# Attention, then a leaky-ReLU MLP, on one core: rebuilding how the attention stage gets its transposed state, its column sums and its evacuations

## Chip, cores, metric

One core of one Trainium2 chip. The metric is the device time of one execution in microseconds (us), median over executions of the same kernel. The engines are named as in the profile: PE (TensorE, the matmuls), ACT (ScalarE), DVE (VectorE), GpSimd, and SyncE, which here only issues transfers. PSUM is where this kernel's matmuls put their results (`ps` in the profile's lines). Before the change: 412.0 us (16 runs, 410.8 to 413.2).

## The reference, cut to what matters

```python
B, H, S, Ns, D = 8, 8, 512, 32, 64           # 64 heads in all
scores  = x @ state.T / 8;  a  = softmax(scores);   xread = a @ state      # (512 x 32) per head
scores2 = state @ x.T / 8;  a2 = softmax(scores2);  sread = a2 @ x         # (32 x 512) per head
tok = concat([xread, sread], axis=2)         # -> 4352 tokens x 512
h = tok @ w_in;  g = max(0.01 * h, h);  out = g @ w_out                    # d_ff = 2048
```

Both softmaxes use the same exponentials, so the kernel computes exp(scores) once per head, in four tiles of 128 tokens.

## The kernel before

Five engine programs with semaphores; the listing is shortened and mostly in comments. Heads run through a software pipeline: step `w` works on head `w` in A, `w-1` in E, and so on.

```python
def dma_hbm_batch(b):      # on GpSimd: x -> xs, state -> ss (both bf16 in HBM), x -> Xbf in SBUF
def dma_sbuf_batch(b):     # on SyncE, nine transfers on one semaphore, sem_in[b]
    # waits for xs[b] and ss[b], then
    #   XTp[c] <- xs, c = 0..3   DMA transpose, 128 x 512
    #   STp[c] <- ss, c = 0..3   DMA transpose, 128 x 32
    #   Sall   <- ss             plain load
# PE, per head:
# A  4 matmuls  scores           (waits sem_in[b] >= 9*16, sem_xbf[b])
# B  4 matmuls  sread numerator  (weights Xbf, 64 columns)
#    4 matmuls  its denominator  (weights ones64, 64 columns)
# C  4 transposes of normalised E2n;  D 1 matmul  xread, 512 columns
# ACT: E 4 exps with accumulator output (the row sums);  G copy ET <- PSUM (32x512 bf16)
# DVE: F reciprocal, product E2n;  H reciprocal and product for sread;  I cast X2T <- PSUM (64x512 fp32)
...
dma_hbm_batch(0); dma_hbm_batch(1); dma_hbm_batch(2)
dma_sbuf_batch(0); dma_sbuf_batch(1)
dma_weights()              # W1 (4 loads) and W2 (4 loads), all at the start
dma_sbuf_batch(2)
for w in range(NH_ALL + 7): # A(w) B(w-2) C(w-3) D(w-5) | E(w-1) G(w-4) | F(w-2) H(w-3) I(w-6)
    ...                    # batch b >= 3 is loaded after D of the last head of batch b-3 (three buffers)
# second stage: per group of 512 tokens 64 matmuls (mm1, L387), leaky ReLU on ACT + DVE, 64 matmuls (mm2, L426)
```

The softmax here doesn't subtract the row's maximum and nothing guards it: scores larger than these inputs give would overflow.

## Time and profile before

| | before |
|---|---|
| time, median | 412.0 us |
| first A (scores matmul of head 0) | 26.0 us |
| last A (head 63) | 160.1 us |
| first matmul of the second stage | 169.2 us |
| second stage | 242.1 us |
| a head, A to A, inside a batch | 1.853 us |

The span is read in two pieces: the attention up to the first mm1 matmul, and the second stage, which the change leaves alone. Inside the attention the starts of A tell everything: the distance from one to the next is the period, and a longer one in front of a batch is a hole. The lines are in the prediction. "x4" after a line of the timeline means that four instructions of a kind are merged into it.

### The profile page before, as it was taken

What the parts mean: (1) busy time and instruction counts of PE and PEld (TensorE: products, weight loads), DVE (VectorE), ACT (ScalarE), POOL (GpSimd) and SP (SyncE); (2) the same over time, 40 slices, a digit from 0 to 9 for tenths busy, and PEclk for the clock granted to TensorE, in tenths of its full rate; (3) what the DMA queues carried; (4) which work ended last, traced back from release to release, by engine and by line L of the source; (5) the groups of instructions that cost most, each with busy time, mean ns of one, the idle gap of its engine ahead of it and who ended that gap; (6) DMA issues with size and microseconds to landing.
All of it is one profiled execution on the core that took longest, in us unless ns stands there. A gap on an engine that the chain in (4) does not pass through costs nothing.

```text
span 411.4 us, 6534 instructions
## 1 busy us (share of the span) xinstructions
PE 356.5 (87%) x2186; PEld 174.4 (42%) x2208; DVE 194.6 (47%) x464; ACT 190.9 (46%) x755; POOL 40.2 (10%) x39
## 2 busy tenths in 40 slices
PE   0046939599689979899999999999999999999996
PEld 0034625365455646233443444434434434344542
DVE  0025838488658868478408137064082270550600
ACT  1045727377557756266326245164262461542511
POOL 7550211221404000000000000000000000000000
DMA  9999999929999900000020110200201101102022
GB/s 67 157 156 198 185 169 128 123 48 141 81 102 83 84 6 2 2 2 0 25 78 0 53 51 1 78 25 24 75 5 41 63 1 60 44 1 77 26 78 76
DMA packets 95425, 26.91 MB, mean 65 GB/s; under 512 B 88224, under 2 KB 90528, under 8 KB 95392
## 3 DMA queue, kind: packets, MB, share of 16 engines
q0 software_dynamic: 70656, 12.85, 38.8%
q1 hardware_dynamic: 24736, 13.64, 14.8%
q8 instruction: 18, 0.29, 0.3%
q14 instruction: 15, 0.12, 0.1%
HBM read 25.95 MB, written 13.37 MB: 96 GB/s over the span
## 4 chain that ended last, share of the span: by engine, by line
PE 73%; SPq 17%; DMA 7%; issue 1%; POOL 1%; DVE 0%; ACT 0%; POOLq 0%; ACTq 0%
PE ps L387 29%; PE ps L426 28%; SPq L166 9%; SPq L172 7%; DMA Sall<-ss 5%; PE ps L297 5%; PE ps L277 4%; PE ps L257 3%; PE ps L215 2%; DMA ss<-in_state_dram 2%; PE ps L264 2%; POOL xs L141 0%; DVE X2T L317 0%; SPq L177 0%; ACT OB L441 0%
## 5 line engine op out<-in xcount | busy, mean ns | idle before, releaser
L408 DVE SCALAR_TENSOR_TENSOR G<-Hs 128x512 bf16<-128x512 bf16 (+1 forms) x144 | 95.4, 663 | 124.4 <-ACT Hs L401 122.8
L387 PE MATMUL ps<-X2T,W 128*128 128x512 bf16 (+1 forms) x565 | 121.9, 373 | 2.1 <-DVE X2T L317 1.4
L426 PE MATMUL ps<-W,G 128*128 128x512 bf16 x533 | 118.0, 379 | 0.6
L401 ACT CAST Hs<-ps 128x512 bf16<-128x512 f32 (+1 forms) x144 | 80.9, 562 | 43.3 <-PE ps L387 42.9
L426 PEld LDWEIGHTS ps<-W,G 128*128 128x128 bf16 x544 | 53.1, 98 | 64.1
L387 PEld LDWEIGHTS ps<-X2T,W 128*128 128x128 bf16 x576 | 48.0, 99 | 75.1 <-ACT Hs L401 36.2
L441 ACT COPY OB<-ps 128x512 f32<-128x512 f32 x34 | 19.9, 585 | 97.7 <-PE ps L426 97.7
L230 ACT ACTIVATE E2s<-ps 128x32 bf16<-128x32 f32 x192 | 35.4, 194 | 58.5 <-PE ps L264 34.1
L215 PE MATMUL ps<-STp,XTp 64*128 64x32 bf16 x256 | 17.9, 189 | 48.0 <-DMA Sall<-ss 48.0
L317 DVE CAST X2T<-ps 64x512 bf16<-64x512 f32 x64 | 43.7, 683 | 2.5 <-PE ps L297 0.4
L290 ACT COPY ET<-ps 32x512 bf16<-32x512 bf16 x64 | 36.7, 573 | 17.5 <-PE ps L297 16.8
L215 PEld LDWEIGHTS ps<-STp,XTp 64*128 64x128 bf16 x256 | 11.5, 104 | 74.1 <-issue 49.6
L297 PE MATMUL ps<-ET,Sall 32*64 32x512 bf16 x64 | 40.1, 630 | 0.4 <-DVE X2T L317 0.4
L277 PE MATMUL ps<-ident,E2n 128*32 128x128 bf16 x256 | 39.0, 308 | 0.0
L247 DVE TENSOR_TENSOR E2n<-E2s,RD 128x128 bf16<-128x128 bf16 x64 | 18.7, 292 | 36.2 <-PE ps L277 35.8
L230 ACT ACTIVATION_READ_ACCUMULATOR E2s<-ps 128x1 f32 x192 | 35.3, 203 | 0.0
L257 PE MATMUL ps<-E2s,Xbf 128*64 128x32 bf16 x256 | 25.2, 219 | 0.6 <-ACT E2s L233 0.6
L141 POOL DMA_DIRECT2D xs<-in_x_dram x8 | 16.6, 2078 | 83.7 <-PE ps L215 81.6
L242 DVE RECIPROCAL RD<-DEN 128x4 bf16<-128x4 f32 x64 | 10.8, 169 | 28.3 <-ACT E2s L233 27.4
L264 PE MATMUL ps<-E2s,ones 128*64 128x32 bf16 x256 | 23.9, 214 | 0.0
L277 PEld LDWEIGHTS ps<-ident,E2n 128*32 128x32 bf16 x256 | 21.9, 129 | 2.8 <-DVE RC L306 0.4
L306 DVE RECIPROCAL RC<-ps 64x32 f32<-64x32 f32 x64 | 21.9, 342 | 0.2 <-PE ps L297 0.2
(18 smaller groups left out, 118.0 us busy)
## 6 DMA issues: line engine op xcount, KB each, us to landing
out_dram<-OB SPq DMA_DIRECT2D x34, 256.0 KB, 2.0
xs<-in_x_dram POOLq DMA_DIRECT2D x8, 512.0 KB, 8.6
Xbf<-in_x_dram POOLq DMA_DIRECT2D x8, 512.0 KB, 10.2
W<-in_moe_w_in_dram POOLq DMA_DIRECT2D x4, 512.0 KB, 20.7
W<-in_moe_w_out_dram POOLq DMA_DIRECT2D x4, 512.0 KB, 31.1
XTp<-xs SPq DMA_TRANSPOSE x32, 4.4
STp<-ss SPq DMA_TRANSPOSE x32, 5.7
...
```

The source lines that it names most:

```text
L166: P_sp.emit(lambda b=b, c=c, bs=bs: sync.dma_start(out=XTp[bs][c].ap(), in_=xs[b][:, c * 128:(c + 1) * 128], transpose=True,).then_inc(sem ...
L215: return pe.matmul(reg_sc(q)[:, 32 * t:32 * t + 32], XTp[bs][ct].ap()[hd:hd + 64, 128 * t:128 * t + 128], STp[bs][ct].ap()[hd:hd + 64, 0:32],)
L230: P_act.emit(lambda t=t, p=p, q=q: act.activation(E2s[p].ap()[:, t, :], reg_sc(q)[:, 32 * t:32 * t + 32], AF.Exp, scale=SCALE, accum_out=D ...
L257: return pe.matmul(reg_srn(q), Xbf[bs].ap()[:, h, t, :], E2s[p].ap()[:, t, :], start=(t == 0), stop=(t == 3))
L277: return pe.transpose(out=reg_et(p)[:, 128 * t:128 * t + 128], in_=E2n[p].ap()[:, t, :], identity=ident.ap(),)
L290: T[i]["etec"] = P_act.mark(lambda p=p: act.copy(ET[p].ap(), reg_et(p)))
L297: T[i]["xrd"] = P_pe.mark(lambda bs=bs, h=h, p=p: pe.matmul(psX[p].ap()[0:64, 0:512], Sall[bs].ap()[:, h, :], ET[p].ap()))
L317: T[i]["xrec"] = P_dve.mark(lambda p=p, ct=ct, hd=hd, tokc=tokc: dve.tensor_copy(X2T[ct].ap()[hd:hd + 64, tokc:tokc + NS], psX[p].ap()[0:6 ...
L387: return pe.matmul(psM1[q].ap()[:, 0:ntok], W1[c].ap()[:, ft * 128:(ft + 1) * 128], X2T[c].ap()[:, tok0:tok0 + ntok], start=(c == 0), stop ...
L401: hc = P_act.mark(lambda q=q, ntok=ntok: act.copy(Hs[q].ap()[:, 0:ntok], psM1[q].ap()[:, 0:ntok]))
L408: e = P_dve.mark(lambda gi=gi, ft=ft, q=q, ntok=ntok: dve.scalar_tensor_tensor(G[gi % 2][ft].ap()[:, 0:ntok], Hs[q].ap()[:, 0:ntok], 0.01, ...
L426: return pe.matmul(psM2[m].ap()[:, 0:512], G[gi % 2][c].ap()[:, rc * 128:rc * 128 + 128], W2[c // 4].ap()[:, c % 4, :], start=(c == 0), st ...
```

## The change

The intent: take the state's transposes off the SyncE queue, let a head wait only for what it needs, and lighten all three compute engines in the attention. In words:

- Sall is loaded straight from HBM by GpSimd; STp is made by a PE transpose of Sall (Tst) and an ACT copy (Q), once per two heads. SyncE issues only the four XTp transposes, each with its own semaphore.
- Xbf gets 64 columns of ones beside its 64 columns of x (Xone), so four matmuls with 128-column weights give numerator and denominator at once.
- One exp of 128 columns per head in place of four with accumulator output; the row sums come from a DVE reduce, and reduce, reciprocal and product run once per two heads.
- The ET copy goes from ACT to DVE, the 64x512 cast from DVE to ACT.
- W2's four loads go from the start to behind batches 3 to 6.
- To make the pairs possible, C runs one step later (`w-4` in place of `w-3`), and H, G and F stand at the front of a step.

The diff is condensed: "..." marks what is cut, and loops are put on one line.

```diff
-        P_sp.wait(sem_ss[b], 16)
         for c in range(4):
-            ...XTp...  .then_inc(sem_in[b], 16))
-        for c in range(4):
-            ...STp[bs][c] <- ss, transpose=True...
-        ...Sall[bs] <- ss...
+            ...XTp...  .then_inc(sem_xt[b][c], 16))
...
+    def grp_Tst(i):                      # PE, even heads
+        T[i]["stt"] = P_pe.mark(... pe.transpose(out=reg_stt(q),
+            in_=Sall[bs].ap()[:, 2 * ct:2 * ct + 2, :], identity=ident.ap()[0:32, 0:32]))
+    def grp_Q(i):                        # ACT
+        T[i]["q"] = P_act.mark(... act.copy(STps[bs][ct].ap(), reg_stt(q)))
...
-        P_pe.wait(sem_in[b], IN_PER_BATCH)
-        P_pe.wait(sem_xbf[b], 16)
+        P_pe.wait(sem_xt[b][ct], 16)
+        P_pe.wait(P_act.sem, ev("q", i - (i % 2)))
...
-        for t in range(4): pe.matmul(reg_srn(q), Xbf[bs].ap()[:, h, t, :], E2s[p].ap()[:, t, :], ...)
-        for t in range(4): pe.matmul(reg_d2r(q), ones64.ap(), E2s[p].ap()[:, t, :], ...)
+        for t in range(4): pe.matmul(reg_sr2(q), Xone[bs].ap()[:, h, t, :], E2s[pp].ap()[:, tk + t, :], ...)
...
-        T[i]["etec"] = P_act.mark(... act.copy(ET[p].ap(), reg_et(p)))
+        T[i]["g"] = P_dve.mark(... dve.tensor_copy(ET[p].ap(), reg_et(p)))
...
-        T[i]["xrec"] = P_dve.mark(... dve.tensor_copy(X2T..., psX[p].ap()[0:64, 0:512]))
+        T[i]["xev"] = P_act.mark(... act.copy(X2T..., psX[p].ap()[0:64, 0:512]))
...
+                if bb < 7:
+                    dma_w2(bb - 3)       # one W2 load behind each of batches 3 to 6
```

More of the change, by code (lines that the diff above doesn't have):

```diff
@@ L8 @@
 ALU = mybir.AluOpType
+AX = mybir.AxisListType
 NB, NH, NS, NSS, ND = 8, 8, 512, 32, 64
@@ L19 @@
 NBANK_C = 4
+NH_ALL = NB * NH
 class _Prog:
@@ L27, in __init__ @@
         self.count = 0
-        self.emitted = 0
         self.ops = []
@@ L32, in emit, with mark @@
         self.ops.append(fn)
-    def ticket(self):
+    def mark(self, fn):
         self.count += 1
-        return self.count
-    def mark(self, fn, ticket=None):
-        if ticket is None:
-            ticket = self.ticket()
-        self.emitted += 1
-        assert ticket == self.emitted, (ticket, self.emitted)
         sem = self.sem
@@ L48, in mark @@
         self.ops.append(_go)
-        return ticket
+        return self.count
     def wait(self, sem, value):
@@ L73, in bass_block_recurrent_cross__then__act_leaky_relu_kernel @@
     ss = nc.dram_tensor("ss", [NB, NSS, D_MODEL], DT.bfloat16)
-    Xbf = [nc.alloc_sbuf_tensor(f"Xbf{i}", [128, NH, 4, ND], DT.bfloat16) for i in range(NBUF_B)]
+    Xone = [nc.alloc_sbuf_tensor(f"Xone{i}", [128, NH, 4, 128], DT.bfloat16) for i in range(NBUF_B)]
+    Sall = [nc.alloc_sbuf_tensor(f"Sall{i}", [NSS, NH, ND], DT.bfloat16) for i in range(NBUF_B)]
     XTp = [[nc.alloc_sbuf_tensor(f"XTp{i}_{c}", [128, NS], DT.bfloat16) for c in range(4)]
            for i in range(NBUF_B)]
-    STp = [[nc.alloc_sbuf_tensor(f"STp{i}_{c}", [128, NSS], DT.bfloat16) for c in range(4)]
-           for i in range(NBUF_B)]
-    Sall = [nc.alloc_sbuf_tensor(f"Sall{i}", [NSS, NH, ND], DT.bfloat16) for i in range(NBUF_B)]
-    E2s = [nc.alloc_sbuf_tensor(f"E2s{i}", [128, 4, 32], DT.bfloat16) for i in range(2)]
-    DEN1 = [nc.alloc_sbuf_tensor(f"DEN1_{i}", [128, 4], DT.float32) for i in range(2)]
-    RD1 = [nc.alloc_sbuf_tensor(f"RD1_{i}", [128, 4], DT.bfloat16) for i in range(2)]
-    E2n = [nc.alloc_sbuf_tensor(f"E2n{i}", [128, 4, 32], DT.bfloat16) for i in range(2)]
-    ET = [nc.alloc_sbuf_tensor(f"ET{i}", [32, 512], DT.bfloat16) for i in range(2)]
+    STps = [[nc.alloc_sbuf_tensor(f"STps{i}_{c}", [128, NSS], DT.bfloat16) for c in range(4)]
+            for i in range(NBUF_B)]
+    E2s = [nc.alloc_sbuf_tensor(f"E2s{i}", [128, 8, 32], DT.bfloat16) for i in range(2)]
+    DEN1 = [nc.alloc_sbuf_tensor(f"DEN1_{i}", [128, 8], DT.float32) for i in range(2)]
+    RD1 = [nc.alloc_sbuf_tensor(f"RD1_{i}", [128, 8], DT.bfloat16) for i in range(2)]
+    E2n = [nc.alloc_sbuf_tensor(f"E2n{i}", [128, 8, 32], DT.bfloat16) for i in range(2)]
+    ET = [nc.alloc_sbuf_tensor(f"ET{i}", [32, NS], DT.bfloat16) for i in range(2)]
     RC2 = [nc.alloc_sbuf_tensor(f"RC2_{i}", [64, 32], DT.float32) for i in range(2)]
-    ones64 = nc.alloc_sbuf_tensor("ones64", [128, 64], DT.bfloat16)
     X2T = [nc.alloc_sbuf_tensor(f"X2T{i}", [128, N_TOK], DT.bfloat16) for i in range(4)]
@@ L106, in reg_sc, with reg_sr2, reg_stt @@
         return psC[q].ap()[:, 0:128]
-    def reg_srn(q):
-        return psC[q].ap()[0:64, 128:160]
-    def reg_d2r(q):
-        return psC[q].ap()[0:64, 160:192]
+    def reg_sr2(q):
+        return psC[q].ap()[:, 128:160]
+    def reg_stt(q):
+        return psC[q].ap()[:, 224:240].bitcast(DT.bfloat16)
     def reg_et(p):
@@ L125, in bass_block_recurrent_cross__then__act_leaky_relu_kernel, with ev @@
     sem_ss = [nc.alloc_semaphore(f"sem_ss{b}") for b in range(NB)]
+    sem_sal = [nc.alloc_semaphore(f"sem_sal{b}") for b in range(NB)]
     sem_xbf = [nc.alloc_semaphore(f"sem_xbf{b}") for b in range(NB)]
-    sem_in = [nc.alloc_semaphore(f"sem_in{b}") for b in range(NB)]
+    sem_xt = [[nc.alloc_semaphore(f"sem_xt{b}_{c}") for c in range(4)] for b in range(NB)]
     sem_ob = [nc.alloc_semaphore(f"sem_ob{i}") for i in range(2)]
-    def ev_of(T, name, i):
+    T = [{} for _ in range(NH_ALL)]
+    def ev(name, i):
         if i < 0:
@@ L133, in ev_of @@
         return T[i][name]
-    P_pool.mark(lambda: pool.memset(ones64.ap(), 1.0))
+    for i in range(NBUF_B):
+        P_dve.mark(lambda i=i: dve.memset(Xone[i].ap()[:, :, :, 64:128], 1.0))
+    N_CONST_EV = P_pool.count
     def dma_hbm_batch(b):
@@ L145, in dma_hbm_batch @@
         P_pool.emit(_xs)
-        def _ss():
-            return pool.dma_start(
-                out=ss[b].rearrange("n (h d) -> n h d", h=NH, d=ND),
-                in_=state[b].rearrange("h n d -> n h d"),
-            ).then_inc(sem_ss[b], 16)
-        P_pool.emit(_ss)
+        P_pool.emit(lambda b=b, bs=bs: pool.dma_start(
+            out=Sall[bs].ap(),
+            in_=state[b].rearrange("h n d -> n h d"),
+        ).then_inc(sem_sal[b], 16))
         def _xbf():
             return pool.dma_start(
-                out=Xbf[bs].ap().rearrange("p h t d -> p (h t) d"),
+                out=Xone[bs].ap()[:, :, :, 0:64].rearrange("p h t d -> p (h t) d"),
                 in_=x[b].rearrange("h (t p) d -> p (h t) d", p=128),
@@ L169, in dma_sbuf_batch @@
                 transpose=True,
-            ).then_inc(sem_in[b], 16))
-        for c in range(4):
-            P_sp.emit(lambda b=b, c=c, bs=bs: sync.dma_start(
-                out=STp[bs][c].ap(),
-                in_=ss[b][:, c * 128:(c + 1) * 128],
-                transpose=True,
-            ).then_inc(sem_in[b], 16))
-        P_sp.emit(lambda b=b, bs=bs: sync.dma_start(
-            out=Sall[bs].ap(),
-            in_=ss[b].rearrange("n (h d) -> n h d", h=NH, d=ND),
-        ).then_inc(sem_in[b], 16))
+            ).then_inc(sem_xt[b][c], 16))
     def dma_weights():
@@ L187, in dma_weights, with dma_w2, head_params @@
             ).then_inc(sem_w1[c], 16))
-        for c in range(4):
-            P_pool.emit(lambda c=c: pool.dma_start(
-                out=W2[c].ap(),
-                in_=moe_w_out[c * 512:(c + 1) * 512, :].rearrange(
-                    "(j p) d -> p j d", p=128),
-            ).then_inc(sem_w2[c], 16))
-    IN_PER_BATCH = 16 * (4 + 4 + 1)
-    NH_ALL = NB * NH
-    T = [{} for _ in range(NH_ALL)]
-    def bidx(i):
-        return i // NH
-    def hidx(i):
-        return i % NH
-    def grp_A(i):
-        b, h = bidx(i), hidx(i)
-        bs, q, hd, ct = b % NBUF_B, i % NBANK_C, (h % 2) * 64, h // 2
-        P_pe.wait(sem_in[b], IN_PER_BATCH)
-        P_pe.wait(sem_xbf[b], 16)
-        P_pe.wait(P_dve.sem, ev_of(T, "srt", i - NBANK_C))
+    def dma_w2(c):
+        P_pool.emit(lambda c=c: pool.dma_start(
+            out=W2[c].ap(),
+            in_=moe_w_out[c * 512:(c + 1) * 512, :].rearrange(
+                "(j p) d -> p j d", p=128),
+        ).then_inc(sem_w2[c], 16))
+    def head_params(i):
+        b, h = i // NH, i % NH
+        return dict(b=b, h=h, bs=b % NBUF_B, ct=h // 2, hd=(h % 2) * 64,
+                    q=i % NBANK_C, p=i % 2, pp=(i // 2) % 2, tk=4 * (i % 2),
+                    s8=i % 8, tokc=b * (NS + NSS))
+    def grp_Tst(i):
+        m = head_params(i)
+        b, bs, ct, q = m["b"], m["bs"], m["ct"], m["q"]
+        P_pe.wait(sem_sal[b], 16)
+        P_pe.wait(P_act.sem, ev("q", i - 4))
+        P_pe.wait(P_dve.sem, ev("srt", i - NBANK_C))
+        P_pe.wait(P_pool.sem, N_CONST_EV)
+        T[i]["stt"] = P_pe.mark(lambda bs=bs, ct=ct, q=q: pe.transpose(
+            out=reg_stt(q), in_=Sall[bs].ap()[:, 2 * ct:2 * ct + 2, :], identity=ident.ap()[0:32, 0:32]))
+    def grp_Q(i):
+        m = head_params(i)
+        b, bs, ct, q = m["b"], m["bs"], m["ct"], m["q"]
+        P_act.wait(P_pe.sem, T[i]["stt"])
+        P_act.wait(P_pe.sem, ev("sc", i - 4))
+        T[i]["q"] = P_act.mark(lambda bs=bs, ct=ct, q=q: act.copy(
+            STps[bs][ct].ap(), reg_stt(q)))
+    def grp_A(i):
+        m = head_params(i)
+        b, bs, hd, ct, q = m["b"], m["bs"], m["hd"], m["ct"], m["q"]
+        P_pe.wait(sem_xt[b][ct], 16)
+        P_pe.wait(P_act.sem, ev("q", i - (i % 2)))
+        P_pe.wait(P_dve.sem, ev("srt", i - NBANK_C))
         def _sc(t):
@@ L217, in _sc @@
                 XTp[bs][ct].ap()[hd:hd + 64, 128 * t:128 * t + 128],
-                STp[bs][ct].ap()[hd:hd + 64, 0:32],
+                STps[bs][ct].ap()[hd:hd + 64, 0:32],
             )
@@ L224, in grp_E @@
     def grp_E(i):
-        p, q = i % 2, i % NBANK_C
+        m = head_params(i)
+        q, pp, tk = m["q"], m["pp"], m["tk"]
         P_act.wait(P_pe.sem, T[i]["sc"])
-        P_act.wait(P_dve.sem, ev_of(T, "e2n", i - 2))
-        P_act.wait(P_pe.sem, ev_of(T, "srd2", i - 2))
-        for t in range(3):
-            P_act.emit(lambda t=t, p=p, q=q: act.activation(
-                E2s[p].ap()[:, t, :], reg_sc(q)[:, 32 * t:32 * t + 32], AF.Exp,
-                scale=SCALE, accum_out=DEN1[p].ap()[:, t:t + 1]))
@@ L233, in grp_E @@
-        T[i]["e2"] = P_act.mark(lambda p=p, q=q: act.activation(
-            E2s[p].ap()[:, 3, :], reg_sc(q)[:, 96:128], AF.Exp,
-            scale=SCALE, accum_out=DEN1[p].ap()[:, 3:4]))
-    def grp_F(i):
-        p = i % 2
-        def _rd1(p=p):
-            with nc.allow_low_precision("bf16 1/den ok"):
-                return dve.reciprocal(RD1[p].ap(), DEN1[p].ap())
-        P_dve.wait(P_act.sem, T[i]["e2"])
-        T[i]["rd1"] = P_dve.mark(_rd1)
-        P_dve.wait(P_dve.sem, T[i]["rd1"])
-        P_dve.wait(P_pe.sem, ev_of(T, "etr", i - 2))
-        T[i]["e2n"] = P_dve.mark(lambda p=p: dve.tensor_mul(
-            E2n[p].ap(), E2s[p].ap(),
-            RD1[p].ap().unsqueeze(2).broadcast_to([128, 4, 32])))
+        P_act.wait(P_dve.sem, ev("e2np", (i // 2) * 2 - 3))
@@ new lines, in grp_E, with grp_F, _rd1 @@
+        P_act.wait(P_pe.sem, ev("srd2", (i // 2) * 2 - 3))
+        T[i]["e2"] = P_act.mark(lambda pp=pp, tk=tk, q=q: act.activation(
+            E2s[pp].ap()[:, tk:tk + 4, :].rearrange("p a b -> p (a b)"),
+            reg_sc(q), AF.Exp, scale=SCALE))
+    def grp_F(j):
+        m = head_params(j)
+        pp = m["pp"]
+        P_dve.wait(P_act.sem, T[j]["e2"])
+        T[j]["rsum"] = P_dve.mark(lambda pp=pp: dve.tensor_reduce(
+            DEN1[pp].ap(), E2s[pp].ap(), AX.X, ALU.add))
+        P_dve.wait(P_dve.sem, T[j]["rsum"])
+        def _rd1(pp=pp):
+            with nc.allow_low_precision("bf16 1/den ok"):
+                return dve.reciprocal(RD1[pp].ap(), DEN1[pp].ap())
+        T[j]["rd1"] = P_dve.mark(_rd1)
+        P_dve.wait(P_dve.sem, T[j]["rd1"])
+        P_dve.wait(P_pe.sem, ev("ctr", j - 4))
+        T[j]["e2np"] = P_dve.mark(lambda pp=pp: dve.tensor_mul(
+            E2n[pp].ap(), E2s[pp].ap(),
+            RD1[pp].ap().unsqueeze(2).broadcast_to([128, 8, 32])))
@@ L251, in grp_B, with _mm @@
     def grp_B(i):
-        b, h = bidx(i), hidx(i)
-        bs, p, q = b % NBUF_B, i % 2, i % NBANK_C
+        m = head_params(i)
+        b, h, bs, q, pp, tk = m["b"], m["h"], m["bs"], m["q"], m["pp"], m["tk"]
+        P_pe.wait(sem_xbf[b], 16)
+        P_pe.wait(P_dve.sem, NBUF_B)
         P_pe.wait(P_act.sem, T[i]["e2"])
-        def _srn(t):
+        def _mm(t):
             return pe.matmul(
-                reg_srn(q), Xbf[bs].ap()[:, h, t, :], E2s[p].ap()[:, t, :],
-                start=(t == 0), stop=(t == 3))
@@ L260, in grp_B @@
-        for t in range(4):
-            P_pe.emit(lambda t=t: _srn(t))
-        def _d2r(t):
-            return pe.matmul(
-                reg_d2r(q), ones64.ap(), E2s[p].ap()[:, t, :],
+                reg_sr2(q), Xone[bs].ap()[:, h, t, :], E2s[pp].ap()[:, tk + t, :],
                 start=(t == 0), stop=(t == 3))
         for t in range(3):
-            P_pe.emit(lambda t=t: _d2r(t))
-        T[i]["srd2"] = P_pe.mark(lambda: _d2r(3))
+            P_pe.emit(lambda t=t: _mm(t))
+        T[i]["srd2"] = P_pe.mark(lambda: _mm(3))
@@ L271, in grp_C @@
     def grp_C(i):
-        p = i % 2
-        P_pe.wait(P_dve.sem, T[i]["e2n"])
-        P_pe.wait(P_act.sem, ev_of(T, "etec", i - 2))
+        m = head_params(i)
+        p, pp, tk = m["p"], m["pp"], m["tk"]
+        podd = (i // 2) * 2 + 1
+        P_pe.wait(P_dve.sem, T[podd]["e2np"])
+        P_pe.wait(P_dve.sem, ev("g", i - 2))
         def _tr(t):
@@ L278, in _tr @@
                 out=reg_et(p)[:, 128 * t:128 * t + 128],
-                in_=E2n[p].ap()[:, t, :],
-                identity=ident.ap(),
-            )
+                in_=E2n[pp].ap()[:, tk + t, :], identity=ident.ap())
         for t in range(3):
             P_pe.emit(lambda t=t: _tr(t))
-        T[i]["etr"] = P_pe.mark(lambda: _tr(3))
+        T[i]["ctr"] = P_pe.mark(lambda: _tr(3))
     def grp_G(i):
-        p = i % 2
-        P_act.wait(P_pe.sem, T[i]["etr"])
-        P_act.wait(P_pe.sem, ev_of(T, "xrd", i - 2))
-        T[i]["etec"] = P_act.mark(lambda p=p: act.copy(ET[p].ap(), reg_et(p)))
-    def grp_D(i):
-        b, h = bidx(i), hidx(i)
-        bs, p = b % NBUF_B, i % 2
-        P_pe.wait(P_act.sem, T[i]["etec"])
-        P_pe.wait(P_dve.sem, ev_of(T, "xrec", i - 2))
-        T[i]["xrd"] = P_pe.mark(lambda bs=bs, h=h, p=p: pe.matmul(
+        m = head_params(i)
+        p = m["p"]
+        P_dve.wait(P_pe.sem, T[i]["ctr"])
+        P_dve.wait(P_pe.sem, ev("xrd", i - 2))
+        T[i]["g"] = P_dve.mark(lambda p=p: dve.tensor_copy(ET[p].ap(), reg_et(p)))
+    def grp_D(i):
+        m = head_params(i)
+        p, bs, h = m["p"], m["bs"], m["h"]
+        P_pe.wait(P_dve.sem, T[i]["g"])
+        P_pe.wait(P_act.sem, ev("xev", i - 2))
+        T[i]["xrd"] = P_pe.mark(lambda p=p, bs=bs, h=h: pe.matmul(
             psX[p].ap()[0:64, 0:512], Sall[bs].ap()[:, h, :], ET[p].ap()))
     def grp_H(i):
-        b, h = bidx(i), hidx(i)
-        p, q, hd, ct = i % 2, i % NBANK_C, (h % 2) * 64, h // 2
-        tokc = b * (NS + NSS)
+        m = head_params(i)
+        q, p, hd, ct, tokc = m["q"], m["p"], m["hd"], m["ct"], m["tokc"]
         P_dve.wait(P_pe.sem, T[i]["srd2"])
-        P_dve.wait(P_dve.sem, ev_of(T, "srt", i - 2))
-        T[i]["rd2"] = P_dve.mark(lambda p=p, q=q: dve.reciprocal(RC2[p].ap(), reg_d2r(q)))
+        P_dve.wait(P_dve.sem, ev("srt", i - 2))
+        T[i]["rd2"] = P_dve.mark(lambda p=p, q=q: dve.reciprocal(
+            RC2[p].ap(), reg_sr2(q)[64:128, :]))
         P_dve.wait(P_dve.sem, T[i]["rd2"])
@@ L309, in grp_H @@
             X2T[ct].ap()[hd:hd + 64, tokc + NS:tokc + NS + NSS],
-            reg_srn(q), RC2[p].ap()))
+            reg_sr2(q)[0:64, :], RC2[p].ap()))
     def grp_I(i):
-        b, h = bidx(i), hidx(i)
-        p, hd, ct = i % 2, (h % 2) * 64, h // 2
-        tokc = b * (NS + NSS)
-        P_dve.wait(P_pe.sem, T[i]["xrd"])
-        T[i]["xrec"] = P_dve.mark(lambda p=p, ct=ct, hd=hd, tokc=tokc: dve.tensor_copy(
+        m = head_params(i)
+        p, hd, ct, tokc = m["p"], m["hd"], m["ct"], m["tokc"]
+        P_act.wait(P_pe.sem, T[i]["xrd"])
+        T[i]["xev"] = P_act.mark(lambda p=p, ct=ct, hd=hd, tokc=tokc: act.copy(
             X2T[ct].ap()[hd:hd + 64, tokc:tokc + NS], psX[p].ap()[0:64, 0:512]))
@@ L321, in bass_block_recurrent_cross__then__act_leaky_relu_kernel @@
     P_pool.mark(lambda: pool.memset(ident.ap(), 0.0))
-    P_pool.wait(P_pool.sem, 2)
+    P_pool.wait(P_pool.sem, P_pool.count)
     P_pool.mark(lambda: pool.affine_select(
@@ L325, in bass_block_recurrent_cross__then__act_leaky_relu_kernel, with okh @@
         pattern=[[-1, 128]], channel_multiplier=1))
-    P_pe.wait(P_pool.sem, 3)
-    dma_hbm_batch(0)
-    dma_hbm_batch(1)
-    dma_hbm_batch(2)
-    dma_sbuf_batch(0)
-    dma_sbuf_batch(1)
-    dma_weights()
-    dma_sbuf_batch(2)
-    for w in range(NH_ALL + 7):
-        if 0 <= w < NH_ALL:
+    N_CONST_EV = P_pool.count
+    for b in range(NBUF_B):
+        dma_hbm_batch(b)
+    for b in range(NBUF_B):
+        dma_sbuf_batch(b)
+    dma_weights()
+    def okh(i):
+        return 0 <= i < NH_ALL
+    for w in range(-1, NH_ALL + 7):
+        if okh(w - 3):
+            grp_H(w - 3)
+        if okh(w - 5):
+            grp_G(w - 5)
+        if okh(w - 2) and (w - 2) % 2 == 1:
+            grp_F(w - 2)
+        if okh(w + 1) and (w + 1) % 2 == 0:
+            grp_Tst(w + 1)
+        if okh(w):
             grp_A(w)
-        if 0 <= w - 2 < NH_ALL:
+        if okh(w - 2):
             grp_B(w - 2)
-        if 0 <= w - 3 < NH_ALL:
-            grp_C(w - 3)
-        if 0 <= w - 5 < NH_ALL:
+        if okh(w - 4):
+            grp_C(w - 4)
+        if okh(w - 5):
             grp_D(w - 5)
-        if 0 <= w - 1 < NH_ALL:
+        if okh(w + 1) and (w + 1) % 2 == 0:
+            grp_Q(w + 1)
+        if okh(w - 1):
             grp_E(w - 1)
-        if 0 <= w - 4 < NH_ALL:
-            grp_G(w - 4)
-        if 0 <= w - 2 < NH_ALL:
-            grp_F(w - 2)
-        if 0 <= w - 3 < NH_ALL:
-            grp_H(w - 3)
-        if 0 <= w - 6 < NH_ALL:
-            grp_I(w - 6)
-        b_first = (w + 1) // NH
-        if (w + 1) % NH == 0 and 3 <= b_first < NB:
-            prev = b_first - NBUF_B
-            last_i = prev * NH + NH - 1
-            P_pool.wait(P_pe.sem, ev_of(T, "xrd", last_i))
-            P_sp.wait(P_pe.sem, ev_of(T, "xrd", last_i))
-            P_sp.wait(P_dve.sem, ev_of(T, "xrec", last_i))
-            dma_hbm_batch(b_first)
-            dma_sbuf_batch(b_first)
+        if okh(w - 6):
+            grp_I(w - 6)
+        if w >= 0 and (w % NH) == 6:
+            bb = w // NH + 2
+            if NBUF_B <= bb < NB:
+                gate = (bb - NBUF_B) * NH + NH - 1
+                P_pool.wait(P_pe.sem, T[gate]["xrd"])
+                P_sp.wait(P_pe.sem, T[gate]["xrd"])
+                dma_hbm_batch(bb)
+                dma_sbuf_batch(bb)
+                if bb < 7:
+                    dma_w2(bb - 3)
     for c in range(4):
```

## The prediction

> **What bounds the kernel now.** I read the page's slices first, then the chain of work that ended last, then PE's waits and its timeline. The slices:
>
> ```profile
> PE   0046939599689979899999999999999999999996
> DMA  9999999929999900000020110200201101102022
> PE 73%; SPq 17%; DMA 7%; issue 1%; POOL 1%; DVE 0%; ACT 0%; POOLq 0%; ACTq 0%
> ```
>
> One slice is 10.3 us. The run has two stages. From slice 17 on (the timeline has the first L387 matmul at 169.24) PE is at 9 without a break: the two big matmuls, 411.4 - 169.2 = 242.1 us, which the change does not touch. Before that comes the attention, 64 heads, where PE is empty for 26 us and has holes at slices 5, 7, 10 and 14 (counted from 0). The chain's SPq 17% + DMA 7% is about 98 us, all of it there, so the holes are on the path that sets the end. The waits and the timeline of PE name them. L215 is A, the first matmul of a head:
>
> ```profile
> PE ps L215 <- DMA Sall<-ss: 48.0, 6, 26.0
> ...
> 26.01 0.53 PE L215 MATMUL ps<-STp,XTp 64*128 64x32 bf16 x12 [26.01 <-DMA Sall<-ss]
> 39.22 0.29 PE L215 MATMUL ps<-STp,XTp 64*128 64x32 bf16 x4 [3.29 <-DMA Sall<-ss]
> 60.53 0.29 PE L215 MATMUL ps<-STp,XTp 64*128 64x32 bf16 x4 [6.41 <-DMA Sall<-ss]
> 80.28 0.29 PE L215 MATMUL ps<-STp,XTp 64*128 64x32 bf16 x4 [4.86 <-DMA Sall<-ss]
> 115.03 0.28 PE L215 MATMUL ps<-STp,XTp 64*128 64x32 bf16 x4 [5.02 <-DMA Sall<-ss]
> 147.14 0.29 PE L215 MATMUL ps<-STp,XTp 64*128 64x32 bf16 x4 [2.40 <-DMA Sall<-ss]
> ```
>
> 48 us of waiting on the last of the nine SyncE transfers of a batch: 26.0 at the start, 22.0 in five holes. Why that transfer is late, SyncE's timeline of batch 4:
>
> ```profile
> 79.05 5.04 SPq L166 DMA_TRANSPOSE XTp<-xs  x4
> 84.13 5.76 SPq L172 DMA_TRANSPOSE STp<-ss  x4
> 89.94 0.58 SPq L177 DMA_DIRECT2D Sall<-ss  x1
> ```
>
> Eight transposes at about 1.26 us of issue each, 11.5 us in a queue, then 5 us to landing (page, part 6). Between the holes PE itself is the bound. One head:
>
> ```profile
> 84.74 0.61 PE L277 MATMUL ps<-ident,E2n 128*32 128x128 bf16 x4
> 85.28 0.63 PE L297 MATMUL ps<-ET,Sall 32*64 32x512 bf16 x1
> 85.84 0.28 PE L215 MATMUL ps<-STp,XTp 64*128 64x32 bf16 x4
> 86.06 0.39 PE L257 MATMUL ps<-E2s,Xbf 128*64 128x32 bf16 x4
> 86.29 0.37 PE L264 MATMUL ps<-E2s,ones 128*64 128x32 bf16 x4
> 86.60 0.61 PE L277 MATMUL ps<-ident,E2n 128*32 128x128 bf16 x4
> ```
>
> Start to start: C (L277) 0.54, D (L297) 0.56, A 0.22, B (L257 and L264) 0.54: 1.85 us a head, no gap, and the starts of A at 82.14 and 96.97 in the timeline are 8 x 1.854 apart. At the end of the stage, where A has run out, the period falls to 1.64, so PE's work sets it. DVE is close behind: in that window 12.47 of 14.83 us busy, ACT 11.16.
>
> [...]
> - [...]49 L387 matmuls take 10.74 us, 219 ns each, in the second stage, but D with the same 512 columns takes 560 ns, and C's four of 128 columns are (0.61 - 0.31) / 3 = 100 ns apart.[...]
> - [...]A's weights have 128 columns, and its four matmuls spread over 0.28 us with a mean of 189 ns, so (0.28 - 0.19) / 3 = 30 ns from one to the next; B's have 64, and (0.39 - 0.22) / 3 = 57 ns.
> - [...](fp32 64x512 from PSUM, 683 ns); no DVE op here reads bf16 from PSUM yet.
> - [...]a transpose lands 3.3 us after issue[...] (window 78.5 to 84) but 15.9 us beside the weights' large packets (window 32.5 to 47).
>
> **The change part by part.**
>
> 1. *Start.* A no longer waits for nine transfers but for one XTp chunk; STp comes from a PE transpose of Sall, and Sall straight from HBM. SyncE issues the first XTp at 10.67; the four of batch 0 landed 6.2 to 7.3 us after issue, so the first is there at 16.9 and the others follow within 5 us, faster than the heads need them. First A at about 17 in place of 26. The first eight heads took 39.22 - 3.3 - 26.0 = 9.9 us while the pipeline filled; with shorter heads about 9. First A of batch 1 (its xs landed in time, SyncE free since 15.5): 26 instead of 39.2. **-13.2 us.** The three memsets of 2048 columns on DVE[...] lie in the empty start.
>
> 2. *The period, PE.* The ones columns in Xone fold the eight matmuls of B into four, with 128-column weights, so they should cost what A's four cost, 0.22 to 0.25, in place of 0.54: -0.30. Tst adds one small matmul with its change of weights per two heads, about 0.1, so 0.05 a head. 1.85 - 0.30 + 0.05 = 1.60.
>
> 3. *The period, DVE.* Now, start to start: RC reciprocal 0.38, its product 0.21, the 64x512 cast 0.72, RD 0.22, E2n 0.20. After: the cast goes to ACT and DVE takes the 32x512 bf16 copy.[...] Per pair of heads: reduce over 256 columns, as E2n's 292 + 128 x 1.04 = 425 ns, with its wait 0.47; RD with eight columns 0.24; E2n on 256 columns 0.33. Sum (2 x (0.38 + 0.21 + 0.46) + 0.47 + 0.24 + 0.33) / 2 = 1.57 a head. Just under PE, and C waits for F only every second step. ACT: one exp of 128 columns[...], one 512-column copy 0.59, half an STp copy 0.10: 0.96, not a bound any more (before: eight records at about 0.09 spacing, plus 0.57).
>  I take 1.63: PE's 1.60 and 0.03 for the uneven steps. 55 heads from batch 1 on: 55 x (1.853 - 1.63) = **-12.3 us**.
>
> 4. *The holes.* A batch's loads wait until D of the last head of the batch three before it, which runs in the fifth step of the batch two before it; its first A stands 16 steps after that batch's start, so 11 steps remain, 18 us at 1.63. Before it needed 9 (xs) + 11.5 + 5 = 25. Now 9 + 1.3 + 3 to 4 = 14. The holes of batches 3 to 7 should close. Left over: XTp of batch 2 and xs of batch 3, which still meet the four W1 loads (they landed by 46.5 in the old run; W2 followed to 60.7 and is now split behind batches 3 to 6). 18.9 us of holes after batch 1 become about 3. **-15.9 us.** W2's 0.5 MB chunks cost each about 3.3 us of DMA; xs and Xbf some 7, XTp some 3: 13 us per batch of 8 x 1.63 = 13.0. It fits, barely.
>
> 5. *Tail and second stage.* From the last A to the first L387 9.1 us now; one step longer per head chain but shorter steps: 9 again. Second stage unchanged.
>
> Sum: 412.2 - 13.2 - 12.3 - 15.9 = 370.8. **371 us.**
>
> **Rivals.**
> - *DVE takes the place of PE.* If the bf16 PSUM copy [...]keeps 0.72 of spacing, and DVE needs (2 x 1.31 + 1.04) / 2 = 1.83 a head: step 3's gain is gone, 371 + 12 = 383. For it: ACT's own copy of the same bf16 data (573 ns) is no faster than from fp32 (585), and DVE already stands at 84%.[...]
> - *The holes stay, under another name.* W2 between the batches shares the DMA engines with XTp, and transposes beside weights took 15.9 us. If the four batches that carry W2 each lose 4 us, 371 + 14 = 385. For it: the fit in step 4 is tight. Against: W2 is queued behind its batch's own xs and Xbf, and the XTp is small.
> [...]
> - *Hidden anyway*: the holes are on the chain, so I give this little.
>
> **Range and chances.** Rivals one and two move the time up by 12 to 14, both at once 26; better steps (1.57, no holes) give 363. 360 to 386 should hold 8 in 10. Even with both rivals the gain is over 3%. Chances: faster 0.97, within 2% 0.02, slower 0.01.
>
> **What would show it.** The first A at about 17 us; A to A 1.6 to 1.65 within batches; the ET copy on DVE near 0.42 us (0.68 means rival one); B's four matmuls 25 to 30 ns apart; PE's waits on DMA after the start under 5 us in all; the first big matmul near 128 us and 242 us from there to the end. Wrong if the period is DVE's, if waits on XTp recur at each batch, or if the second stage waits for W2.

Two terms below it have lost their working: the 0.46 us of the ET copy, in DVE's 1.57, and the exp's 0.27 us, in ACT's 0.96 and no longer printed. Both were estimates; the profile after shows 412 ns for the copy and 278 ns for the exp. That DVE stays under PE's 1.60 rested on the first. Also cut are the length of the memsets, what was said against the first rival, and a third rival, PE's matmuls becoming faster in a denser stream, with 371 - 3 = 368; the 363 of the range takes its 1.57 from it. The 1.04 ns a column is (683 - 183) / 480, from DVE's operations on 512 and 32 columns in the trace before. Estimates are also the 0.1 us for Tst and, in step 4, the 3.3, 7 and 3 us of DMA, which are 0.5, 1 and 0.5 MB at the 157 GB/s of the page's second slice. "Large packets" are those of the window 32.5 to 47, where 514 of 3375 packets were of 2 KB or more; in the window 78.5 to 84 none of 5102 was. That W2 and XTp get in each other's way shows as time: the first chunks of batches 4 and 5 took 7.2 and 7.8 us with W2 between the batches and 5.2 and 4.2 without.

## The result, and the profile after

The changed kernel takes 373.2 us (median of 9 runs; the eight fast ones lie between 372.3 and 374.6 us), 0.906 of the time before (95% interval 0.905 to 0.908). A ratio is the mean time of one kernel's fast runs over that of the other's fast runs of the same rounds, so it is not quite the ratio of the medians quoted here. The remaining run, which was the profiled one, was slow (491 us, mean granted clock 0.748: 1.00 until 131 us, 0.76 from 131 to 140, 0.65 from 140 on), so the kernel was profiled again; everything below is from that second profile (373.7 us, 4 runs, ratio 0.908).

| | before | changed |
|---|---|---|
| first A | 26.0 | 16.5 |
| first A of batch 1 | 39.2 | 27.1 |
| last A | 160.1 | 121.2 |
| first matmul of the second stage | 169.2 | 129.8 |
| second stage | 242.1 | 241.7 |
| span of the profiled run | 411.4 | 371.5 |

The page's slices of the changed kernel, now 9.3 us each:

```profile
PE   0089499999999899999999999999999999999996
DMA  9999999999990000002002002002002011011012
```

PE has one hole left, at slice 4 (counted from 0). The DMA engines, which had a quiet slice in the attention before and were busy until about 144 us, now stay at 9 through slice 11, about 111 us, until all loads are done. The waits of PE (us in total, times, longest):

```profile
PE ps L212 <- DMA XTp<-xs: 12.8, 4, 5.8
PE ps L193 <- DMA Sall<-in_state_dram: 10.5, 1, 10.5
```

L212 is A and L193 the new transpose Tst. The start is 10.5 us for Sall and 5.8 more for the first XTp chunk; 7.0 us of waiting are left for the whole rest, where there were 22. Firsts of the batches, from the timeline of PE (start, duration, instruction, in brackets the idle time and what ended it):

```profile
16.54 0.28 PE L212 MATMUL ps<-STps,XTp 64*128 64x32 bf16 x4 [5.79 <-DMA XTp<-xs]
27.10 0.28 PE L212 MATMUL ps<-STps,XTp 64*128 64x32 bf16 x4
45.39 0.28 PE L212 MATMUL ps<-STps,XTp 64*128 64x32 bf16 x4 [5.37 <-DMA XTp<-xs]
...
84.34 0.28 PE L212 MATMUL ps<-STps,XTp 64*128 64x32 bf16 x4 [0.20 <-DMA XTp<-xs]
```

Five holes have become one of 5.4 us, in front of batch 2, and a trace of one in front of batch 5. Two heads of the steady part, with the engines mixed:

```profile
100.41 0.28 PE L212 MATMUL ps<-STps,XTp 64*128 64x32 bf16 x4
...
100.62 0.29 PE L257 MATMUL ps<-E2s,Xone 128*128 128x32 bf16 x4
...
100.85 0.61 PE L272 MATMUL ps<-ident,E2n 128*32 128x128 bf16 x4
...
101.39 0.63 PE L291 MATMUL ps<-ET,Sall 32*64 32x512 bf16 x1
101.49 0.41 DVE L284 COPY ET<-ps 32x512 bf16<-32x512 bf16 x1
...
101.95 0.20 PE L193 MATMUL ps<-ident,Sall 32*128 32x32 bf16 x1
...
102.08 0.28 PE L212 MATMUL ps<-STps,XTp 64*128 64x32 bf16 x4
...
103.62 0.28 PE L212 MATMUL ps<-STps,XTp 64*128 64x32 bf16 x4
```

Start to start: A 0.21, B 0.23 (it was 0.54), C 0.54, D 0.56, and 0.13 for Tst in every second head. A to A is 1.67 and 1.54, so 1.605 a head on average. The busy times of the stretch from 90 to 110 us say which engine that is:

```profile
90.00:110.00 20.00, 20.00 (x166) 10.70 (x164) 17.58 (x58) 11.39 (x32) 4.28 (x3) 1.00 1.64 150
```

The columns after the length are PE, PE weight loads, DVE, ACT, GpSimd, then granted clock, DMA share and GB/s: PE is busy in all 20 us, DVE in 17.6, ACT in 11.4. DVE is not far behind: from one pair of heads to the next (3.21 us) the timeline shows it waiting 0.18 to 0.19 us for PE, which leaves a need of about 1.51 us a head (estimate) against PE's 1.605.

### The profile page after: what moved, and what is told of

Read it like the earlier page. It is cut to its first block, busy times and chain, and to the rows that moved or that the text cites. A ratio compares the mean times of both kernels' runs of the same rounds, so it can differ in the third digit from the quotient of the medians.

```text
span 488.9 us, 5714 instructions
## 1 busy us (share of the span) xinstructions
PE 456.4 (93%) x1962; PEld 190.7 (39%) x1984; DVE 191.0 (39%) x435; ACT 159.2 (33%) x339; POOL 40.2 (8%) x38
## 4 chain that ended last, share of the span: by engine, by line
PE 87%; DMA 8%; POOL 2%; issue 2%; DVE 1%; ACT 0%; POOLq 0%; DVEq 0%
PE ps L386 36%; PE ps L425 36%; PE ps L291 5%; PE ps L272 5%; DMA XTp<-xs 5%; DMA xs<-in_x_dram 3%; PE ps L212 2%; PE ps L257 2%; POOL xs L139 1%; POOL Xone L151 1%; PE ps L193 1%; DVE ET L284 0%; ACT X2T L310 0%; POOL Sall L145 0%; DVE RC L299 0%
## 5 line engine op out<-in xcount | busy, mean ns | idle before, releaser
L386 PE MATMUL ps<-X2T,W 128*128 128x512 bf16 (+1 forms) x565 | 178.2, 495 | 2.5 <-ACT X2T L310 1.2
L425 PE MATMUL ps<-W,G 128*128 128x512 bf16 x533 | 177.3, 513 | 1.6 <-issue 0.6
L386 PEld LDWEIGHTS ps<-X2T,W 128*128 128x128 bf16 x576 | 68.4, 121 | 111.1 <-issue 82.8
L440 ACT COPY OB<-ps 128x512 f32<-128x512 f32 x34 | 19.9, 585 | 157.9 <-PE ps L425 157.9
L310 ACT CAST X2T<-ps 64x512 bf16<-64x512 f32 x64 | 37.0, 578 | 13.6 <-PE ps L291 12.9
L212 PE MATMUL ps<-STps,XTp 64*128 64x32 bf16 x256 | 18.1, 189 | 12.9 <-DMA XTp<-xs 12.9
L284 DVE COPY ET<-ps 32x512 bf16<-32x512 bf16 x64 | 26.3, 412 | 1.9 <-PE ps L272 0.9
L212 PEld LDWEIGHTS ps<-STps,XTp 64*128 64x128 bf16 x256 | 11.5, 103 | 27.7 <-DMA XTp<-xs 15.6
L257 PE MATMUL ps<-E2s,Xone 128*128 128x32 bf16 x256 | 18.6, 193 | 0.0
L193 PE MATMUL ps<-ident,Sall 32*128 32x32 bf16 x32 | 6.4, 201 | 12.1 <-DMA Sall<-in_state_dram 10.5
L227 ACT ACTIVATE E2s<-ps 128x128 bf16<-128x128 f32 x64 | 17.4, 277 | 0.7
L151 POOL DMA_DIRECT2D Xone<-in_x_dram x8 | 16.2, 2021 | 5.0 <-issue 5.0
L245 DVE TENSOR_TENSOR E2n<-E2s,RD 128x256 bf16<-128x256 bf16 x32 | 13.6, 425 | 1.1
## 6 DMA issues: line engine op xcount, KB each, us to landing
W<-in_moe_w_in_dram POOLq DMA_DIRECT2D x4, 512.0 KB, 18.9
```

Source lines behind the costliest of these rows:

```text
L212: return pe.matmul(reg_sc(q)[:, 32 * t:32 * t + 32], XTp[bs][ct].ap()[hd:hd + 64, 128 * t:128 * t + 128], STps[bs][ct].ap()[hd:hd + 64, 0:32],
L257: return pe.matmul(reg_sr2(q), Xone[bs].ap()[:, h, t, :], E2s[pp].ap()[:, tk + t, :], start=(t == 0), stop=(t == 3))
L284: T[i]["g"] = P_dve.mark(lambda p=p: dve.tensor_copy(ET[p].ap(), reg_et(p)))
L310: T[i]["xev"] = P_act.mark(lambda p=p, ct=ct, hd=hd, tokc=tokc: act.copy(X2T[ct].ap()[hd:hd + 64, tokc:tokc + NS], psX[p].ap()[0:64, 0:512]))
L386: return pe.matmul(psM1[q].ap()[:, 0:ntok], W1[c].ap()[:, ft * 128:(ft + 1) * 128], X2T[c].ap()[:, tok0:tok0 + ntok], start=(c == 0), stop ...
L425: return pe.matmul(psM2[m].ap()[:, 0:512], G[gi % 2][c].ap()[:, rc * 128:rc * 128 + 128], W2[c // 4].ap()[:, c % 4, :], start=(c == 0), st ...
```

## The experiments

My theory had two halves: the chain of transfers sets when a batch starts, and PE's own instructions set the period in between. The rivals: that the period is DVE's or ACT's, or a loop of waits; that the two halves add up as independent parts; and, for each single part of the change, that it was hidden anyway. All ten kernels gave correct results. Times are medians of 4 runs. The kernel before, timed in the same rounds, had medians of 411.5, 411.7 and 411.2 us in the three sittings. The first sitting (the first four rows) ran on another chip than the two later ones, so the ratio is the safer column to compare by.

| kernel | us | ratio to before | A to A | holes after the start |
|---|---|---|---|---|
| changed kernel again | 373.7 | 0.908 | 1.605 | 5.4 at batch 2 |
| new engine program, old transfers | 404.5 | 0.982 | 1.54 | 32 in five |
| old engine program, new transfers | 389.8 | 0.947 | 1.92 | 2.7 at batch 2 |
| without the fold of B | 389.8 | 0.947 | 1.92 | about 3 at batch 2 |
| evacuations back on their old engines | 383.9 | 0.933 | 1.83 | 4.2 at batch 2 |
| W2 at the start | 382.3 | 0.929 | 1.605 | batches 2 and 3 |
| A waits for four chunks | 381.7 | 0.929 | 1.62 | batches 2, 4, 6 |
| four exps, no reduce | 372.7 | 0.907 | 1.605 | 5 at batch 2 |
| all weights behind batch 7 | 374.2 | 0.909 | 1.605 | 6 at batch 7 |
| the same, after its transposes | 366.8 | 0.892 | 1.605 | none |

### The changed kernel once more

> The changed kernel once more, for a profile in the fast state. Every theory expects about 373 us, a granted clock of 1.00 throughout, the first matmul of the second stage near 130 us, 242 us from there to the end, and A to A of 1.54 and 1.67 us in turn, with one hole of about 5.6 us before batch 2.

As expected in every point; its lines are shown above.

### New engine program with the old transfers

```diff
-        ...Sall[bs] <- state...           -> sem_sal     # and Tst, Q
+        ...ss[b] <- state...              -> sem_ss
+        P_sp.wait(sem_ss[b], 16)
+        ...4 x STps[bs][c] <- ss, transpose; Sall[bs] <- ss...  -> sem_in[b]
-        P_pe.wait(sem_xt[b][ct], 16)
-        P_pe.wait(P_act.sem, ev("q", i - (i % 2)))
+        P_pe.wait(sem_in[b], 16 * 9)
+    for c in range(4): dma_w2(c)          # at the start, not behind batches 3 to 6
```

> The new engine program with the old transfers: state through HBM, eight transposes and Sall on SyncE, A waits for all nine, W2 at the start. My theory, that the old transfer chain sets the start of each batch: first A at 26, batch 1 at 39, batch 2 at 60, then a batch starts 4.5 heads plus 25 us after the batch two before it, that is every 16 us, though its work takes 12.9; last A near 155, end 404 to 409: a gain of only 4 to 8 us of the 39. Rival A, the shorter PE period pays by itself, 63 x 0.25 = 16 us: 396. Rival B, parts add up with the transfers worth little: under 390.

Measured 404.5 us, inside my 404 to 409; 7 us better than before, not the 16 of rival A. The interval of the ratio, 0.979 to 0.984, lies clear of 1 but on both sides of a gain of 2%. Firsts of batches, from the timeline of PE (A is L222 here):

```profile
38.65 0.28 PE L222 MATMUL ps<-STps,XTp 64*128 64x32 bf16 x4 [4.15 <-DMA Sall<-ss]
59.30 0.28 PE L222 MATMUL ps<-STps,XTp 64*128 64x32 bf16 x4 [8.27 <-DMA Sall<-ss]
78.65 0.29 PE L222 MATMUL ps<-STps,XTp 64*128 64x32 bf16 x4 [6.97 <-DMA Sall<-ss]
110.95 0.28 PE L222 MATMUL ps<-STps,XTp 64*128 64x32 bf16 x4 [7.59 <-DMA Sall<-ss]
140.35 0.28 PE L222 MATMUL ps<-STps,XTp 64*128 64x32 bf16 x4 [4.69 <-DMA Sall<-ss]
```

The same five holes as before, and each is longer (4.15 against 3.29, 8.27 against 6.41, and so on): together 31.7 us where the kernel before had 22.0. The period is 0.31 us shorter per head, almost 20 us over 63 heads, and the holes take 10 of them back. (The trace is of the fastest of the four runs, at 402.9 us; the median gains 3 us less than these two terms.) A batch that is done sooner only waits longer for the next nine transfers.

### Old engine program with the new transfers

```diff
-        ...4 x STp <- ss, transpose; Sall <- ss...       # on SyncE
+        ...Sall[bs] <- state...                          # on GpSimd
+        grp_Tst (PE) and grp_Q (ACT) as in the change; one semaphore per XTp chunk
+        W2 behind batches 3 to 6;  H ahead of F on DVE
```

> The old engine program with the new transfers: Sall straight from HBM, STp from a transpose on PE and a copy on ACT, one semaphore per XTp chunk, W2 behind batches 3 to 6. H goes ahead of F on DVE so that the PE transpose can stand a step early. My theory: first A at 16.6, A to A 1.85 + 0.06, one hole of 2 to 5 us at batch 2, the others closed: last A near 135, end 386 to 392, a gain of 20 to 26. Rival A, the holes were PE's and DVE's lag and not the queue's: 400 or more. If the two parts were independent, this gain and that of the new engine program alone would sum to 39; my theory has them sum to about 29, because the shorter period makes holes of the time it saves as long as the old transfers stay.

Measured 389.8 us: the gain of 21.7 was expected at 20 to 26. One hole is left, at batch 2:

```profile
46.93 0.28 PE L224 MATMUL ps<-STp,XTp 64*128 64x32 bf16 x4 [2.75 <-DMA XTp<-xs]
```

With the run above this makes a square: 411.5 before, 404.5 and 389.8 with one half each, 373.7 with both. The halves alone save 7.0 + 21.7 = 28.7 us, both save 37.8. The 9 us between are what the new engine program loses to the holes as long as the old transfers stand. The rival of independent parts falls.

### Without the fold of B

```diff
-                reg_sr2(q), Xone[bs].ap()[:, h, t, :], E2s[pp].ap()[:, tk + t, :],
+                reg_srn(q), Xone[bs].ap()[:, h, t, 0:64], E2s[pp].ap()[:, tk + t, :],      # 4 of these
+                reg_d2r(q), Xone[bs].ap()[:, h, t, 64:128], E2s[pp].ap()[:, tk + t, :],    # and 4 of these
```

> The changed kernel with B's four matmuls with 128-column weights undone into eight with 64, all else kept. My theory, PE sets the period: A to A from 1.61 to 1.89 to 1.92 us, time 373 + 63 x 0.29 = 391, less a part of the hole of batch 2, so 386 to 392. Rival, DVE (1.42 busy) or a loop of waits sets the period: under 380.

Measured 389.8 us, in the range. In the timeline of PE, A to B, B to its second half, and that to C:

```profile
100.79 0.28 PE L215 MATMUL ps<-STps,XTp 64*128 64x32 bf16 x4
101.00 0.39 PE L260 MATMUL ps<-E2s,Xone 128*64 128x32 bf16 x4
101.23 0.37 PE L267 MATMUL ps<-E2s,Xone 128*64 128x32 bf16 x4
101.54 0.61 PE L282 MATMUL ps<-ident,E2n 128*32 128x128 bf16 x4
```

B is back at 0.54, and the periods are 1.85 and 1.99: exactly PE's sum plus Tst (in every second step), while DVE was busy for only 14.7 of 20 us:

```profile
90.00:110.00 20.00, 20.00 (x182) 12.40 (x180) 14.71 (x48) 9.01 (x25) 7.12 (x6) 1.00 1.59 130
```

Same period and same time as the old engine program with the new transfers, though ACT's and DVE's work differs between the two: with eight matmuls in B, the merged exp, the pairing and the exchange of evacuations together are worth nothing (they were not taken apart here; that PE has no idle time says why). Of the new engine program it is the fold that pays; the question is whether the rest is needed once it has.

### Evacuations back on their old engines

```diff
-        T[i]["g"]   = P_dve.mark(... dve.tensor_copy(ET[p].ap(), reg_et(p)))
+        T[i]["g"]   = P_act.mark(... act.copy(ET[p].ap(), reg_et(p)))
-        T[i]["xev"] = P_act.mark(... act.copy(X2T..., psX[p].ap()[0:64, 0:512]))
+        T[i]["xev"] = P_dve.mark(... dve.tensor_copy(X2T..., psX[p].ap()[0:64, 0:512]))
```

> The changed kernel with the two evacuations back on their old engines: the ET copy on ACT, the 64x512 fp32 cast on DVE; the fold stays. The prediction's account: DVE then needs (2 x (0.38 + 0.21 + 0.72) + 1.04) / 2 = 1.83 us a head against PE's 1.61, so the period becomes about 1.83 and the time 384 to 388 (63 x 0.22 = 14, less up to 3 of the hole of batch 2). Rival: the swap is worth nothing, since eight matmuls of B gave the same 1.92 with either distribution (the runs without the fold and with the transfers alone): 373 to 375.

Measured 383.9 us, at the near edge of the expected 384 to 388; the period is 1.53 and 2.14 in turn, 1.83 on average, the figure worked out. PE's stretch from 90 to 110 us, and the pause that comes once per two heads:

```profile
90.00:110.00 20.00, 17.59 (x147) 9.53 (x148) 18.54 (x51) 9.37 (x28) 4.28 (x3) 1.00 1.82 148
```

```profile
98.27 0.18 PE L193 MATMUL ps<-ident,Sall 32*128 32x32 bf16 x1 [0.40 <-DVE X2T L302]
```

PE now idles and DVE is at 93%, its instructions one behind the other: they set the period through Tst, which the program lets wait for the sread product that reads the same PSUM tile. The 1.83 came out of terms that were off both ways, though: the product over two heads takes 0.46 us start to start, where 0.33 was predicted; the reduce takes 0.43 (predicted 0.47), and the sread product before it 0.11 (0.21). So the exchange is worth nothing before the fold and 10 us after it: it keeps DVE from becoming the bound that the fold would have uncovered.

### Four exps again, without the reduce

```diff
-        ...one act.activation over 128 columns...
+        for t in range(4): act.activation(E2s[..., tk + t], ..., accum_out=DEN1[pp].ap()[:, tk + t:tk + t + 1])
-        T[j]["rsum"] = P_dve.mark(... dve.tensor_reduce(DEN1[pp].ap(), E2s[pp].ap(), AX.X, ALU.add))
```

> The changed kernel with the one exp per head undone into four with accumulator output, and without the reduce on DVE: ACT goes from 0.96 to about 1.45 to 1.6 us a head, DVE loses 0.23. My theory, PE's 1.61 stays the bound: 373 to 376. Rival, ACT with its gaps becomes the bound: 380 or more.

Measured 372.7 us with an unchanged period. Merging the exps is hidden: undoing it cost no time (ratio 0.907 against 0.908), so ACT, busy for 11.4 of 20 us in the changed kernel, has room for the four, and DVE is rid of the reduce (396 ns per two heads there).

### W2 back at the start

```diff
     dma_weights()
+    for c in range(4): dma_w2(c)
-                if bb < 7: dma_w2(bb - 3)
```

> The changed kernel with the four W2 loads back at the start, behind W1. If large weight packets delay transposes and the next xs, the chunks of batch 2 land at about 45, 50, 55, 58 and xs of batch 3 near 64, so batch 3 starts near 68 in place of 58: 381 to 385. Rival: moving W2 is hidden anyway: 373 to 375.

Measured 382.3 us, in the range. Batch 3 starts at 67.8 in place of 58.3. Moving W2 is worth 9 us of the change.

### A waits for all four chunks

```diff
-        P_pe.wait(sem_xt[b][ct], 16)
+        for c in range(4): P_pe.wait(sem_xt[b][c], 16)
```

> The changed kernel, but A waits for all four XTp chunks of its batch and not for its own. My theory, the chunks matter at the start (first A 21.5 in place of 16.5) and wherever the transfers run close (the last chunk of batch 4 landed at 75.2, its first A was at 71.4): hole at batch 2 grows by 4.6 and holes of some 3 us come at batches 4 to 7: 378 to 386. Rival, one semaphore per chunk is cosmetic: 373 to 375.

Measured 381.7 us, in the range; first A at 21.7, and holes at batches 2, 4 and 6 (three steps of 9.5, 3.2 and 4.0 us from one A to the next; the trace is of the slowest of the four runs, at 384.3 us), where I had expected small ones at each of 4 to 7. The split semaphore is worth 8 us: the first chunk of a batch is in time where the last is not.

### All weights behind batch 7

```diff
-    dma_weights()                                  # W1, at the start
-                if bb < 7: dma_w2(bb - 3)
+                if bb == 7:
+                    dma_weights()
+                    for c in range(4): dma_w2(c)
-        P_pe.wait(sem_w2[c], 16)                   # before the second stage
+        if gi == 1: ...P_pe.wait(sem_w2[c], 16)    # before the first matmul that reads W2
```

> The changed kernel with all eight weight loads behind batch 7, and the wait for W2 moved to the first matmul that reads it. If the hole of 5.4 us before batch 2 is W1's doing, it closes, and W1 lands near 115, before the second stage at 124: 366 to 369. Rival A, the hole is the lateness of xs of batch 2 (landed 30.9): it stays, 373. Rival B, the second stage then waits for weights: 374 or more, with a wait on the weights ahead of its first matmul.

Missed: 374.2 us. The hole at batch 2 did close (batch 2 started at 39.8, where it had been 45.4), so W1 was its cause and the lateness of xs was not. (W2 moved in this run too, but in the changed kernel the first transpose of batch 2 was issued at 30.9 and W2's first load only at 39.4, when that transpose would long have landed at the 2.8 to 5.0 us seen without weights.) But the same hole came back at batch 7, whose transposes now run beside the weights:

```profile
110.26 0.29 PE L212 MATMUL ps<-STps,XTp 64*128 64x32 bf16 x4 [6.14 <-DMA XTp<-xs]
```

I had checked when the weights would land and forgotten what they do to the transposes queued next to them.

### The weights only after batch 7's transposes

```diff
                 if bb == 7:
+                    for c in range(4): P_pool.wait(sem_xt[7][c], 16)
                     dma_weights()
```

> As the run with all weights behind batch 7, but GpSimd issues them only when the four XTp chunks of batch 7 have landed (near 98). The hole that moved to batch 7 should go too: firsts of the batches at 16.4, 27, 40, 53, 65, 78, 91, 104, last A near 115.5, first matmul of the second stage near 124, W1 landed by 113, W2 by 127: 366 to 369, about 1.4% better than the changed kernel. Rival: the hole has another cause than weights beside transposes and stays somewhere: 372 or more.

Measured 366.8 us, ratio 0.892: better than both kernels, 6.9 us under the changed one. No hole is left, the last A is at 115.0 and the first matmul of the second stage at 123.6, within 1 us of what was expected; W1 landed by 116 and W2 by 127, before they were read. From issue to landing of XTp chunks, for those issued from 29 to 44 us, first in the changed kernel, then in this one:

```profile
DMA to landing us min/median/max: 7.7/13.9/14.5
```

```profile
DMA to landing us min/median/max: 2.8/3.9/5.0
```

The second line is of five transposes (the fifth is the first of batch 3), the first of four. At batch 7 the same comparison is 15.2 to 19.9 us beside the weights and 2.7 to 4.6 ahead of them.

## Why the prediction was right

The predicted 371.0 us stand against 373.2 measured, in the range of 360 to 386. By its own steps, with the span of the profiled runs shorter by 39.9 us:

| step | predicted | measured | from |
|---|---|---|---|
| 1 start, to first A of batch 1 | -13.2 | -12.1 | 39.2 to 27.1 |
| 2 and 3 period, 55 heads | -12.3 | -13.6 | 1.853 to 1.605 |
| 4 holes after batch 1 | -15.9 | -13.1 | 18.7 to 5.6 |
| 5 tail | 0 | -0.6 | 9.1 to 8.6 |
| 5 second stage | 0 | -0.5 | 242.1 to 241.7 |
| sum | -41.4 | -39.9 | |

The sum is closer than its terms: the start fell short by 1.1 us and the period gave 1.3 us more than predicted, which cancel by luck. The holes fell short by 2.8 us, and tail and second stage gave 1.1 back.

- *Start.* The first A came at 16.5, predicted 17. Batch 1 began 1.1 later than predicted: the second chunk did not come faster than the heads need it, as step 1 had it, and the first eight heads lost a little: in the timeline PE idles 1.40 us for the second chunk and, at the two Tst that follow, 0.86 and 0.68 us for DVE's product of four heads before, which reads the same PSUM tile. The memsets took 1.77 us each and were hidden as predicted.
- *PE's period.* 1.60 predicted, 1.605 measured. B's slot is 0.23 (predicted 0.22 to 0.25), Tst's 0.13 per two heads (0.1). The 0.03 added for uneven steps was not needed: DVE's pile-up in odd steps never reached PE. Without the fold the period is 1.92, Tst's share above the kernel before, so all of this term is the fold's.
- *DVE's period.* The ET copy (32x512, bf16 from PSUM) took 412 ns, near the 0.42 us predicted, where the fp32 cast (64x512) took 683 in the kernel before; so the first rival, a copy that keeps the cast's 0.72 of spacing, is out. That DVE would need 1.83 a head with the old evacuation could not be seen in the changed kernel; putting it back gave 1.83. In the changed kernel DVE's need was about 1.51, predicted 1.57. The 1.04 ns a column held for E2n, which went from 292 to 425 ns with 128 more columns; the reduce over 256 columns took 396 ns (predicted 425).
- *Holes.* Those of batches 3 to 7 closed. The remainder was put at about 3 us and was 5.6, all but 0.2 of it at batch 2: the mis-sized term. The prediction named the place and W1 as its cause, and holding the weights back closed it. The others closed with nothing to spare. Step 4 said of the DMA time that it fits, barely, but its time plan showed 4 us of slack: it gave a batch 14 us from the issue of xs to its first XTp chunk and 18 us of room. For batch 5 xs was issued at 66.8 and landed 9.6 us later, and the first chunk then took 7.8 us in place of 3 to 4: it landed at 84.3, after 17.5 us, and PE had waited 0.2 us. Batch 4's chunk took 7.2 us. With no W2 between the batches (the last experiment) the first chunks of batches 4 and 5 took 5.2 and 4.2 us, and the whole way 13.9 and 12.6. So the second rival, W2 costing each of its batches about 4 us, did happen (3.4 and 4.9 us by these two), and the slack hid it.
- *PE's matmuls* did not become faster in the attention: the 512-column D still takes 0.56 us start to start and C's 128-column transposes are still about 100 ns apart, with PE busy for 20.00 of 20 us and a granted clock of 1.00, where the 512-column matmuls of the second stage took 219 ns each in the kernel before (49 in 10.74 us). What makes the difference, no run shows.
- *Signs and sums.* Of the signs it named, three were missed by a little: PE waited 7.0 us on DMA after the start (under 5 predicted), B's matmuls are 33 ns apart (25 to 30), and the second stage begins at 129.8 (128). Its 18.9 us of holes after batch 1 are 18.7 by its own lines, and its better case, 363, is 364.5 by its own terms (370.8 - 55 x 0.06 - 3).
- *What the prediction did not say:* that the halves depend on each other, and that the merged exp is hidden. Both were shown only by the experiments.

One thing stays open: how much of the fold's gain is fewer matmuls and how much their closer spacing: B's pairs of weight load and matmul are (0.29 - 0.19) / 3 = 33 ns apart with 128-column weights and (0.39 - 0.22) / 3 = 57 ns with 64. The two were changed together in every run.
